# One-bank PSUM tiles and coefficients spread by a product, in a kernel of channel attention and two gated layers

## The chip, the cores and the metric

One core of a Trainium2 chip runs the kernel. The metric is the device time of one execution in microseconds. The engines are PE (matrix products), DVE (vector), ACT (scalar functions), POOL (general) and SP, which only issues loads and stores; each runs its own list of instructions in order. Products write to PSUM, which has eight banks of 512 fp32 columns; everything else lies in SBUF.

## The reference

q, k and v are 6016 x 256. q and k are normalised by column, a 256 x 256 softmax mixes the channels of v, and two layers with a nonlinear gate follow.

```python
qn = q / (np.linalg.norm(q, axis=1, keepdims=True) + 1e-06)
kn = k / (np.linalg.norm(k, axis=1, keepdims=True) + 1e-06)
s = kn.transpose(0, 2, 1) @ qn / tau
a = softmax(s)                       # a /= a.sum(-1) + 1e-09
x = v @ a                            # 6016 x 256
h = x @ w_in                         # 256 -> 2048
P = a[0] + a[1]*h + a[2]*h**2 + a[3]*h**3
Q = 1.0 + abs(b[0])*abs(h) + abs(b[1])*h**2
y = (P / (Q + 1e-06)) @ w_out        # 2048 -> 256
out = (sigmoid(y @ w_gate) * (y @ w_val)) @ w_out2   # 256 -> 1536 -> 256
```

## The kernel before

The weights arrive as 64-bit numbers. Each of 17 pieces (`win0` to `win3`, `wo0` to `wo3`, `wg0` to `wg2`, `wv0` to `wv2`, `wo20` to `wo22`) is loaded, converted to fp32 (`to_f32`: ACT at L710, a shift by DVE at L717 or ACT at L713, a merge of bits by DVE at L721) and split into a high and a low part (`split`: L796 or L800, and the subtraction at L803 by DVE or POOL). Three products of parts then stand for one in fp32.

**Loading.** q and k come in 15 chunks of 2, 4 or 1 tiles of 128 rows (names `<-in_kqk_dram`), into buffers that a weight will take later. PE adds the scores up in `s_ps` (tag `pO`, L489); ACT squares (L510), DVE and POOL add squares (L519), and PE adds them over the rows by products with `ones` into `nrm` (L458). The three coefficient vectors b, tau and a are loaded by SP as broadcasts to 128 partitions (L530), and DVE prepares them (`coefs`, `coefs_a`, L535 to L551).

**Norms and softmax.** DVE adds the sums (L571), ACT takes the root, DVE makes the reciprocals and two diagonal matrices (L584); PE spreads these over the partitions by products with `ones` (L591), DVE copies the result (L593) and makes scaled scores with their maxima (L605), ACT the exponentials, DVE the scale (L622): the weights e (`e_sb`). PE then transposes e (L650) and multiplies the first 384 tokens of v by it (L635, `x_ps`). Filler products that nobody reads (L663, `WARM` of them) keep PE busy.

**Fold.** For the other tokens e is multiplied into w_in: eight units, two to each piece of `win`, of eight instructions each on PE (L754, `w_mm`). ACT evacuates a unit's high part (L766), DVE subtracts for the low part (L768).

**Blocks.** The tokens are worked in 12 blocks, the first of 384, the others of 512. The first layer has eight steps (`moe1`): two first-layer products into `pH` or `pO` (block 0 in plain fp32, L882; later blocks in parts, L872 to L876), the gate on ACT and DVE (u, |h|, h squared, a reciprocal by seed and arctangent; Q at L903, t at L911, y at L916, g at L919), and second-layer products into `pY` (L929 in block 0, L947 to L957 later). `moe2` follows per block (L993 to L1030) beside the next block's first layer.

**PSUM.** Tags `pH`, `pY`, `pO` are tiles of two banks, `pG` and `pV` of one. Until the first product of `moe2`, `pG` and `pV` are the two halves of a single two-bank tile `gv` (class `Half`); then `part_gv` gives it up and opens a pool for each. The norms, the norm product, the fillers, the transposes and the fold units go to these two halves, and in three of block 0's eight steps (`S0`) the squared term `S_` is both halves of `gv` at once. Dependencies are found by tile: an instruction that touches one half of `gv` waits for the users of the other.

**Order.** A planner (`Plan.schedule`) lists the instructions of each engine by modelled ready times and by due times; the tables `VT0`, `VT1`, `VT`, `WT`, `ORDER` and the letter strings set the due times, the order of loads, which engine does a conversion, and which PSUM tile it goes through.

```python
def part_gv():                                        # L343
    if pools["pG"].pool is None:
        both.close()
        for tag in ("pG", "pV"):
            pools[tag].pool = ctx.enter_context(tc.tile_pool(name="r_" + tag, bufs=depth[tag], space=PSUM))
...
for x, lo_, n, k in ((b, 4, 2, "b"), (tau, 6, 1, "t"), (a, 0, 4, "a")):        # L529
    pl.op(SP, .2, -9999.0 + CF_AT["bta".index(k)], lambda x=x, lo_=lo_, n=n: nc.sync.dma_start(
        out=sm[:, lo_:lo_ + n], in_=bcast(x, n)), (), ["sm_" + k], tail=2.0)
```

Of the kernel before, what the change touches and what calls it, by code (L numbers as in the profile page):

```python
# [9 lines left out]
F32 = mybir.dt.float32  # L10
# [4 lines left out]
ALU = mybir.AluOpType  # L15
PSUM = bass.MemoryType.PSUM
# [17 lines left out]
PE, ACT, DVE, POOL, SP = "PE", "ACT", "DVE", "POOL", "SP"  # L34
# [30 lines left out]
WARM = 6  # L65
PLC = (-1, 3, 6, -1, 3, -1, 5, 3, 7, 0, 4, -1, -1, 3, -1)
# [6 lines left out]
TOP = 'adaaaaaddaaddadad'  # L73
HI = 'dadadaadddaaa'
LOW = 'pdppdpdpppppp'


T_PS = 'HYYYH..HYY.YYYY..'
# [12 lines left out]
ET_PS = 'G'  # L91
ET_EV = 'd'
# [184 lines left out]
def tile_channel_attention_two_moes(  # L277
# [14 lines left out]
    nc = tc.nc  # L292
# [30 lines left out]
    class Half:  # L323

        def __init__(self, tag):
            self.tag, self.pool = tag, None

        def tile(self, shape, dtype, tag=None, name=None):
            if self.pool is None:
                return gv[:, "GV".index(self.tag[1]), :]  # L330
            return self.pool.tile(shape, dtype, tag=tag, name=name)

    for tag, n in depth.items():
        if tag in ("pG", "pV"):
            pools[tag] = Half(tag)
            continue
        kw = {"space": PSUM} if tag[0] == "p" else {}
        pools[tag] = ctx.enter_context(tc.tile_pool(name="r_" + tag, bufs=n, **kw))

    both = ctx.enter_context(ExitStack())  # L340
    gv = both.enter_context(tc.tile_pool(name="r_gv", bufs=1, space=PSUM)).tile([P, 2, NB], F32, name="gv")

    def part_gv():  # L343
        if pools["pG"].pool is None:
            both.close()
            for tag in ("pG", "pV"):
                pools[tag].pool = ctx.enter_context(tc.tile_pool(name="r_" + tag, bufs=depth[tag], space=PSUM))
# [178 lines left out]
    def bcast(src, n):  # L526
        return src.rearrange("(o n) -> o n", o=1).broadcast_to([P, n])
# [153 lines left out]
    def to_f32(vt, wt, c, rkey, dst, key, n, how, t_ps, stay=False):  # L681
# [163 lines left out]
    def moe1(b_, y_ps, nat, vhi, vlo, j):  # L845
# [18 lines left out]
        def V(x):  # L864
            return (gv if x is None else x.ap())[:, :, :n]

        for i in range(2):
# [37 lines left out]
            [a_] + S_, [a_], port=not free_s)  # L905
# [69 lines left out]
    def moe2(b_, yhi, ylo):  # L975
# [7 lines left out]
        for f in range(F2):  # L983
# [120 lines left out]
```

## Time and profile before

| | |
|---|---|
| three runs, us | 1220.6, 1221.65, 1222.77 (median 1221.65) |
| the profiled execution, us | 1221.94, span of its instructions 1220.1 |
| mean granted clock of PE | 0.992 |
| busy us: PE, DVE, ACT, POOL | 1186.0, 965.0, 837.8, 510.2 |
| HBM read and written | 36.31 and 6.16 MB |
| loads and stores of SP and ACT | 35 GB/s over the span, but 342, 388 and 272 in the first three slices of 1/40 |

The span runs from the first to the last instruction. A duration in a row is that of the instruction itself; matrix products are pipelined, so a row's products overlap by some 0.1 to 0.2 us with the next row's. The idle time before an instruction is put down to whatever ended it last. On PE a product in fp32 appears as two records.

### The profile page before, as it was taken

To read this page: it belongs to the slowest core of one execution; us is meant where nothing else is said; L and a number is where in the kernel's file an instruction comes from. 1 tells how busy PE (TensorE), PEld (TensorE's weight loads), DVE (VectorE), ACT (ScalarE), POOL (GpSimd) and SP (SyncE) were. 2 spreads that over 40 slices of the span, in tenths; PEclk is the share of its full clock that TensorE was granted. 3 is DMA by queue.
4 is the path that set the end of the run, shared out by engine and by line. 5 is a ranking of instruction groups with operands and counts; after the bars stand their busy time and mean duration, and the time that the engine had idled before them with its cause. 6 is when DMAs were issued, how large, how long until landed. Compare 5 with 4: busy or idle time off the path is not lost.

```text
span 1220.1 us, 13195 instructions
## 1 busy us (share of the span) xinstructions
PE 1186.0 (97%) x5182; PEld 967.6 (79%) x5182; DVE 965.0 (79%) x841; ACT 837.8 (69%) x984; POOL 510.2 (42%) x261
## 2 busy tenths in 40 slices
PE   7978999999999999999999999999999999999998
PEld 5755588888788888888888888888888888888877
DVE  3878988578789789789789889888888878878811
ACT  4787777567677677677677677677677677667622
POOL 2602344444345345345345345345335435435422
PEclk9979999999999999999999999999999999999999
DMA  8970000000100100100100100000000000000000
GB/s 342 388 272 18 18 1 1 31 1 1 35 1 1 35 1 1 35 1 1 35 1 1 35 1 1 27 9 1 18 18 0 18 19 1 18 1 1 18 1 18
DMA packets 15614, 43.32 MB, mean 36 GB/s; under 512 B 1344, under 2 KB 1856, under 8 KB 14272
## 3 DMA queue, kind: packets, MB, share of 16 engines
q1 hardware_dynamic: 15408, 42.21, 9.3%
q8 instruction: 41, 0.67, 0.2%
q10 hardware_dynamic: 144, 0.26, 0.1%
q14 instruction: 21, 0.17, 0.0%
HBM read 36.31 MB, written 6.16 MB: 35 GB/s over the span
## 4 chain that ended last, share of the span: by engine, by line
PE 89%; DVE 5%; DMA 4%; ACT 1%; issue 1%; SPq 0%; DVEq 0%; ACTq 0%
PE pO L1022 10%; PE pY L949 7%; PE pY L947 7%; PE pH L872 6%; PE pH L874 6%; PE pH L876 6%; PE pY L957 6%; PE pG L993 5%; PE pV L993 5%; PE pG L995 5%; PE pV L995 5%; PE pV L997 5%; PE pG L997 5%; PE pO L1030 5%; DMA win<-in_kqk_dram 2%; PE pO L489 1%
## 5 line engine op out<-in xcount | busy, mean ns | idle before, releaser
L1015 POOL TENSOR_TENSOR lo<-sig,hi 128x512 fp32r<-128x512 f32 (+1 forms) x143 | 246.5, 1730 | 333.3 <-ACT hi L1011 333.3
L939 POOL TENSOR_TENSOR lo<-w,hi 128x1024 fp32r<-128x1024 f32 x88 | 216.8, 2463 | 276.9 <-ACT hi L934 229.3
L916 DVE SCALAR_TENSOR_TENSOR a<-a,s 128x1024 f32<-128x1024 f32 (+1 forms) x93 | 162.4, 1748 | 57.5 <-ACT a L913 57.5
L893 ACT ACTIVATE a<-pH,cf 128x1024 f32<-128x1024 f32 (+1 forms) x92 | 101.7, 1106 | 98.5 <-PE pH L876 98.5
L903 DVE SCALAR_TENSOR_TENSOR a<-a,s 128x1024 f32<-128x1024 f32 (+1 forms) x93 | 112.7, 1212 | 49.7 <-ACT s L895 48.1
L1022 PE MATMUL pO<-hi,wo 128*128 128x512 f32 (+1 forms) x580 | 151.5, 383 | 0.0
L913 ACT ACTIVATE a<-a 128x1024 f32<-128x1024 f32 (+1 forms) x96 | 100.0, 1042 | 62.5 <-DVE a L911 61.3
L1008 DVE TENSOR_TENSOR sig<-sig,pV 128x512 f32<-128x512 f32 (+2 forms) x145 | 96.6, 667 | 57.7 <-PE pV L997 54.0
L919 DVE SCALAR_TENSOR_TENSOR w<-w,cf,a 128x1024 f32<-128x1024 f32 (+1 forms) x95 | 138.2, 1456 | 2.9
L947 PE MATMUL pY<-hi,wo 128*128 128x512 f32 x352 | 137.9, 392 | 2.3 <-ACT hi L934 2.3
L872 PE MATMUL pH<-vhi,win 128*128 128x512 f32 x352 | 137.3, 390 | 0.8 <-DVE w L900 0.8
L949 PE MATMUL pY<-hi,wo 128*128 128x512 f32 x352 | 138.0, 392 | 0.0
L911 DVE TENSOR_TENSOR a<-a,s 128x1024 f32<-128x1024 f32 (+1 forms) x89 | 137.9, 1549 | 0.0
L874 PE MATMUL pH<-vlo,win 128*128 128x512 f32 x352 | 137.1, 390 | 0.0
L876 PE MATMUL pH<-vhi,win 128*128 128x512 f32 x352 | 137.1, 389 | 0.0
L1011 ACT ACTIVATE hi<-sig 128x512 fp32r<-128x512 f32 (+2 forms) x145 | 90.3, 623 | 66.1 <-DVE sig L1008 65.8
L1022 PEld LDWEIGHTS pO<-hi,wo 128*128 128x128 f32 x580 | 108.1, 188 | 21.1
L900 DVE SCALAR_TENSOR_TENSOR w<-w,cf,pH 128x1024 f32<-128x1024 f32 (+1 forms) x92 | 116.5, 1266 | 1.7
L993 PE MATMUL pG<-yhi,wg 128*128 128x512 f32 (+1 forms) x288 | 112.1, 389 | 1.6 <-ACT yhi L968 1.1
L995 PE MATMUL pG<-ylo,wg 128*128 128x512 f32 (+1 forms) x288 | 111.2, 386 | 1.5 <-DVE ylo L970 1.5
L1006 ACT ACTIVATE sig<-pG 128x512 f32<-128x512 f32 (+2 forms) x145 | 85.3, 589 | 38.7 <-PE pG L997 24.2
L993 PE MATMUL pV<-yhi,wv 128*128 128x512 f32 (+1 forms) x288 | 111.6, 388 | 0.0
(214 smaller groups left out, 2323.7 us busy)
## 6 DMA issues: line engine op xcount, KB each, us to landing
wo<-in_moe_w_out_dram SPq DMA_DIRECT2D x7, 1024.0 KB, 13.2
v<-in_v_dram SPq DMA_DIRECT2D x11, 512.0 KB, 3.7
out_dram<-v SPq DMA_DIRECT2D x10, 512.0 KB, 2.8
win<-in_kqk_dram SPq DMA_DIRECT2D x4, 1024.0 KB, 14.4
win<-in_moe_w_in_dram SPq DMA_DIRECT2D x4, 1024.0 KB, 8.6
wv<-in_moe_w_val_dram SPq DMA_DIRECT2D x3, 1024.0 KB, 14.1
wo<-in_kqk_dram SPq DMA_DIRECT2D x3, 1024.0 KB, 19.7
wg<-in_moe_w_gate_dram SPq DMA_DIRECT2D x3, 1024.0 KB, 13.8
```

Source lines behind the costliest of these rows:

```text
L872: mm(out=hp.ap()[:, i, :n], lhsT=WIN.at(f * P, 0, z), rhs=vhi.ap()[:, z, :n], start=(z == 0), stop=False)
L874: mm(out=hp.ap()[:, i, :n], lhsT=WIN.at(f * P, 0, z), rhs=vlo.ap()[:, z, :n], start=False, stop=False)
L876: mm(out=hp.ap()[:, i, :n], lhsT=WIN.at(f * P, 1, z), rhs=vhi.ap()[:, z, :n], start=False, stop=(z == 1))
L916: pl.op(DVE, c_dve(N), vt + vp['y'] * d, lambda: stt(out=V(y_), in0=V(a_), scalar=ATAN_C, in1=V(s_), op0=ALU.add, op1=ALU.mult), [a_] + S_ ...
L919: pl.op(DVE, c_dve(N, 1), vt + vp['g'] * d, lambda: stt(out=V(w_), in0=V(w_), scalar=col(A0), in1=V(y_), op0=ALU.add, op1=ALU.mult), [w_, ...
L939: lambda: e_lo.tensor_tensor(out=V(lo), in0=V(w_), in1=V(hi).bitcast(F32), op=ALU.subtract),
L947: mm(out=y_ps.ap()[:, z, :n], lhsT=WO.at(f * C, 0)[:, sl], rhs=hi.ap()[:, i, :n], start=(f == 0), stop=False)
L949: mm(out=y_ps.ap()[:, z, :n], lhsT=WO.at(f * C, 1)[:, sl], rhs=hi.ap()[:, i, :n], start=False, stop=False)
L993: mm(out=gp[i].ap()[:, :n], lhsT=wt.at(f * P, 0, z), rhs=yhi.ap()[:, z, :n], start=(z == 0), stop=False)
L995: mm(out=gp[i].ap()[:, :n], lhsT=wt.at(f * P, 0, z), rhs=ylo.ap()[:, z, :n], start=False, stop=False)
L1015: lambda sg=sg, hi=hi, lo=lo, sl=sl, e=e: e.tensor_tensor(out=lo.ap()[:, sl], in0=sg.ap()[:, sl], in1=hi.ap()[:, sl].bitcast(F32), op=ALU. ...
L1022: mm(out=o_ps.ap()[:, z, sl], lhsT=WO2.at(f * C, i)[:, z * P:(z + 1) * P], rhs=hi.ap()[:, sl], start=(f == 0 and i == 0), stop=False)
```

## The change

`Half`, `gv` and `part_gv` go: `pG` and `pV` are pools of one-bank tiles from the start, so the norms, the norm product, the fillers, the transposes and each fold unit have tiles of their own. The squared term of block 0 always lies in SBUF (`S0`, `W0` go). The coefficients are loaded by ACT as rows into partition 0 of a zeroed tile `row`; one product with `ones` spreads them over the partitions, and DVE copies eight columns. The tables are replaced (`WT`, `VT0`, `VT1`, `UNIT`, `PLC` and others), with twelve fillers instead of six, and the transposes go to a `pO` tile that ACT evacuates.

```diff
-ORDER = 'xx2xvxxxgxvxxxxxgxxoxoiioiongvi22'
+ORDER = 'xx2xxxxxxxgxvvxxogxxxoiiio2nogvi2'
...
-KG = 'ggssssssssssgsg'
+KG = 'ggsssssssssssgs'
...
-S0 = 'sssgsgsg'
-T0 = 'pdpdpppd'
+T0 = 'pdpdpddp'
...
-WARM = 6
+WARM = 12
...
-F_PS = 'VVGGVVGG'
-CF_AT = (4.3, 4.4, 24.5)
+F_PS = 'VVGGVGGV'
...
-ET_PS = 'G'
-ET_EV = 'd'
+ET_PS = 'O'
+ET_EV = 'a'
...
-    class Half:
...
-    both = ctx.enter_context(ExitStack())
-    gv = both.enter_context(tc.tile_pool(name="r_gv", bufs=1, space=PSUM)).tile([P, 2, NB], F32, name="gv")
-
-    def part_gv():
...
-    for x, lo_, n, k in ((b, 4, 2, "b"), (tau, 6, 1, "t"), (a, 0, 4, "a")):
-        pl.op(SP, .2, -9999.0 + CF_AT["bta".index(k)], lambda x=x, lo_=lo_, n=n: nc.sync.dma_start(
-            out=sm[:, lo_:lo_ + n], in_=bcast(x, n)), (), ["sm_" + k], tail=2.0)
+    row = const.tile([P, 8], F32, name="row")
+    pl.op(POOL, .2, t_s - 1, lambda: nc.gpsimd.memset(row, 0.0), (), ["row"], port=True)
+    for x, lo_, n, k in ((a, 0, 4, "a"), (b, 4, 2, "b"), (tau, 6, 1, "t")):
+        pl.op(ACT, .1, -30000.0, lambda x=x, lo_=lo_, n=n: nc.scalar.dma_start(
+            out=row[0:1, lo_:lo_ + n], in_=x.rearrange("(o n) -> o n", o=1)), ["row"], ["row_" + k], tail=9.0)
+    c_ps = pl.buf("pG", [P, 512], at=t_s)
+    pl.op(PE, .1, -30000.0, lambda: mm(out=c_ps.ap()[:, 0:8], lhsT=ones, rhs=row, start=True, stop=True),
+          ["ones", "row", "row_a", "row_b", "row_t"], [c_ps])
+    pl.op(DVE, .2, -30000.0, lambda: nc.vector.tensor_copy(sm[:, 0:8], c_ps.ap()[:, 0:8]), [c_ps],
+          ["sm_a", "sm_b", "sm_t"])
...
-        free_s = b_ == 0 and S0[j] == "g"
-        if free_s:
-            S_ = [pl.buf("pG", [P, 512], at=at), pl.buf("pV", [P, 512], at=at)]
-            s_ = None
-        else:
-            s_ = pl.buf("s", [P, 2, NB], at=at)
-            S_ = [s_]
+        s_ = pl.buf("s", [P, 2, NB], at=at)
+        S_ = [s_]
```

Three places of the lists follow; a number behind a name is that of the buffer, and L numbers are those of each kernel's own file. The start of PE's list: products of the scores (`pO`) and of the sums (`gv` or `pV`, out of `s` and `a`), and the spreading of `row`. Before:

```order
L489 MATMUL pO_134<-wg0_126 128x384 x4
L458 MATMUL gv_112<-ones_114,s_132 128x1 x4
L489 MATMUL pO_134<-wv1_128 128x384 x4
L458 MATMUL gv_112<-ones_114,a_139 128x1 x4
L489 MATMUL pO_134<-win0_141 128x256 x8
```

Now:

```order
L464 MATMUL pO_141<-wo20_133 128x384 x4
L433 MATMUL pV_156<-ones_116,s_139 128x1 x4
L507 MATMUL pG_164<-row_119,ones_116 128x8
L464 MATMUL pO_141<-wv0_135 128x384 x4
L433 MATMUL pV_156<-ones_116,a_148 128x1 x4
L464 MATMUL pO_141<-wo0_137 128x256 x8
```

The product of the coefficients stands between the first and the second chunk.

SP's list around the last chunks of q and k (`in_kqk_dram`). Before:

```order
L413 DMA wv2_309<-in_kqk_dram 128x2048
L413 DMA win3_317<-in_kqk_dram 128x512
L413 DMA wo0_321<-in_moe_w_out_dram 128x4x512
L413 DMA wo22_340<-in_kqk_dram 128x512
L413 DMA wo1_343<-in_moe_w_out_dram 128x4x512
L413 DMA wg1_361<-in_moe2_w_gate_dram 128x2x1024
L413 DMA win1_379<-in_kqk_dram 128x512
```

Now:

```order
L388 DMA wo0_303<-in_moe_w_out_dram 128x4x512
L388 DMA wg1_314<-in_moe2_w_gate_dram 128x2x1024
L388 DMA wv1_329<-in_moe2_w_val_dram 128x2x1024
L388 DMA wo2_344<-in_kqk_dram 128x2048
L388 DMA wv2_355<-in_kqk_dram 128x512
L388 DMA wg2_360<-in_kqk_dram 128x512
L388 DMA win1_365<-in_kqk_dram 128x512
```

Seven weights stood ahead of the last chunk, now six do.

PE's list from the sums to the first products of block 0: the norm product (out of `w` and `ones`, 128x128), fillers (128x256), the transposes (with `ident`), the product with v (`v` and `a`), fold units (`hi` or `vhi` with `v`), and first-layer products (out of `vlo`). Before:

```order
L591 MATMUL gv_112<-w_418,ones_114 128x128 x2
L663 MATMUL gv_112<-w_418,ones_114 128x256 x6
L650 MATMUL gv_112<-ident_113,a_479 128x128 x4
L635 MATMUL pH_510<-v_463,a_479 128x384 x4
L754 MATMUL gv_112<-hi_434,v_513 128x256 x4
L754 MATMUL gv_112<-vhi_454,v_513 128x256 x4
L882 MATMUL pH_549<-vlo_530,hi_434 128x384 x2
L754 MATMUL gv_112<-hi_434,v_513 128x256 x4
```

Now:

```order
L570 MATMUL pG_466<-w_439,ones_116 128x128 x2
L642 MATMUL pV_473<-w_439,ones_116 128x256 x6
L614 MATMUL pH_504<-v_470,a_479 128x384 x4
L629 MATMUL pO_519<-ident_115,a_479 128x128 x4
L642 MATMUL pV_473<-w_439,ones_116 128x256
L854 MATMUL pH_533<-vlo_524,hi_452 128x384 x2
L731 MATMUL pG_541<-vhi_487,v_529 128x256 x4
L854 MATMUL pH_533<-vlo_524,hi_452 128x384 x2
L854 MATMUL pO_560<-vlo_524,hi_452 128x384 x4
```

The product with v has moved ahead of the transposes, the first first-layer products ahead of the fold, and the names of the tiles differ from unit to unit; five more fillers follow further down.

## Rows read from the trace of the kernel before

**Rows 1.** Stretches: length, busy us (instructions) by engine, PE's clock, DMA share, GB/s.

```profile
12.00:18.00 6.00, 5.15 (x27) 4.12 (x25) 0.38 (x3) 3.74 (x5) 2.36 (x1) 1.00 0.67 235
18.00:58.00 40.00, 34.77 (x157) 29.53 (x158) 29.69 (x31) 28.25 (x30) 23.93 (x10) 1.00 1.01 404
58.00:64.50 6.50, 6.50 (x48) 5.98 (x46) 6.10 (x9) 5.81 (x6) 0.09 (x1) 0.90 0.80 269
64.50:77.70 13.20, 7.20 (x21) 5.25 (x21) 9.10 (x28) 9.43 (x13) 0.00 (x0) 0.53 1.01 395
77.70:83.80 6.10, 6.10 (x24) 4.64 (x25) 4.11 (x4) 4.84 (x6) 2.74 (x1) 1.00 0.96 358
83.80:112.30 28.50, 22.43 (x81) 14.51 (x79) 21.10 (x26) 22.45 (x29) 6.83 (x3) 1.00 0.07 23
112.30:148.70 36.40, 34.73 (x108) 20.19 (x109) 36.05 (x39) 29.36 (x37) 11.87 (x6) 1.00 0.05 15
227.00:1220.10 993.10, 983.70 (x4314) 809.31 (x4312) 791.61 (x647) 673.13 (x789) 425.69 (x213) 1.00 0.03 12
```

The engines in a row stand in the order PE, PE's weight loads, DVE, ACT, POOL.

**Rows 2.** Loads and stores: who issues, count, KB each, us from issue to landing.

```profile
out_dram<-v ACTq DMA_DIRECT2D x1, 256.0 KB, 2.1
sm<-in_moe_b_dram SPq DMA_DIRECT2D x1, 1.0 KB, 13.7
...
sm<-in_moe_a_dram SPq DMA_DIRECT2D x1, 2.0 KB, 8.1
```

**Rows 3.** PE in order of time: start, duration, line, product, records, [idle before <-releaser].

```profile
9.98 2.83 PE L489 MATMUL pO<-wv 128*128 128x384 f32 x8
...
40.35 3.62 PE L489 MATMUL pO<-wo 128*128 128x256 f32 x16
...
57.70 1.45 PE L489 MATMUL pO<-wo 128*128 128x384 f32 x4
...
63.50 0.99 PE L458 MATMUL gv<-ones,s 128*128 128x1 f32 x4
69.74 1.22 PE L591 MATMUL gv<-w,ones 128*128 128x128 f32 x4 [5.25 <-DVE w L584]
...
72.33 4.63 PE L663 MATMUL gv<-w,ones 128*128 128x256 f32 x10 [0.52 <-DVE w L593]
...
77.67 2.85 PE L635 MATMUL pH<-v,a 128*128 128x384 f32 x8 [0.24 <-DVE hi L721]
80.35 1.89 PE L754 MATMUL gv<-hi,v 128*128 128x256 f32 x8
...
83.81 1.45 PE L882 MATMUL pH<-vlo,hi 128*128 128x384 f32 x4
...
143.12 5.43 PE L929 MATMUL pY<-w,hi 128*128 128x384 f32 x16 [0.62 <-DVE w L919]
```

**Rows 4.** DVE in order of time, from the sums to block 0's last gate product.

```profile
66.51 0.17 DVE L542 TENSOR_SCALAR cf<-sm 128x4 f32<-128x4 f32 x1 [1.81 <-DMA sm<-in_moe_a_dram]
...
71.86 0.42 DVE L593 COPY w<-gv 128x256 f32<-128x256 f32 x1 [1.91 <-PE gv L663]
72.20 1.22 DVE L721 SCALAR_TENSOR_TENSOR lo<-pY,win 128x1024 int32<-128x1024 int32 x1
...
76.13 0.35 DVE L622 TENSOR_SCALAR a<-a,sm 128x256 f32<-128x256 f32 x1
...
143.97 1.02 DVE L919 SCALAR_TENSOR_TENSOR w<-w,cf,gv 128x768 f32<-128x768 f32 x1
```

**Rows 5.** DVE by line, 76 to 145 us: busy, mean ns | idle before, releasers.

```profile
L768 DVE TENSOR_TENSOR win<-gv,win 128x512 fp32r<-128x512 f32 x8 | 5.5, 689 | 7.8 <-PE gv L754 4.1 <-ACT win L766 3.0 <-ACT wo L713 0.7
L916 DVE SCALAR_TENSOR_TENSOR a<-a,s 128x768 f32<-128x768 f32 x5 | 4.7, 950 | 0.0
```

**Rows 6.** DVE in order of time: two instructions that run beside POOL.

```profile
55.74 3.43 DVE L721 SCALAR_TENSOR_TENSOR ylo<-ylo,wo 128x1024 int32<-128x1024 int32 x1 [0.15 <-ACT wo L713]
...
177.31 2.04 DVE L911 TENSOR_TENSOR a<-a,s 128x1024 f32<-128x1024 f32 x1
```

More of the change, by code (lines that the diff above doesn't have):

```diff
@@ L49 @@
 LOADS = (2, 2, 4, 4, 4, 4, 4, 4, 4, 4, 4, 4, 1, 1, 1)
-KG = 'ggssssssssssgsg'
-UNIT = 'ddpddpdpddpppppddppdddppdpddppp'
+KG = 'ggsssssssssssgs'
+UNIT = 'dppppdpddpppdppddpppddpdpppdpdp'
 IN_TMP = ('hi', 'vhi', 'lo', 'lo')
-TMP = ('yhi', 'ylo', 'v', 'hi', 'lo', 'v', 's', 'vlo', 'vhi', 'v', 's', 'w', 'lo')
-LO0 = 'dpdppdpd'
-S0 = 'sssgsgsg'
-T0 = 'pdpdpppd'
+TMP = ('yhi', 'ylo', 'v', 'hi', 'vhi', 'v', 's', 'w', 'w', 'hi', 'ylo', 'a', 'hi')
+LO0 = 'dppppddp'
+T0 = 'pdpdpddp'
 HAM = 0.5
 SUM_AT = 1
-WARM = 6
@@ L66 @@
-PLC = (-1, 3, 6, -1, 3, -1, 5, 3, 7, 0, 4, -1, -1, 3, -1)
+WARM = 12
+PLC = (0, 2, -1, 7, 0, 6, -1, 2, -1, -1, -1, 6, -1, 7, 2)
 ACTIVE = 0.5
@@ L70 @@
 DEPTH = {'w': 3, 'a': 3, 's': 2, 'hi': 2, 'lo': 2, 'sig': 2, 'hi2': 2, 'lo2': 2, 'yhi': 1, 'ylo': 1, 'vhi': 1, 'vlo': 1, 'v': 2, 'pH': 1, 'pG': 1, 'pV': 1, 'pY': 1, 'pO': 1}
[L73 to L78, printed above, removed]
+TOP = 'aaaadadddddaaadad'
+HI = 'dddaaaaadddda'
+LOW = 'ddpdppppppddp'
+T_PS = 'YYYY.H..HY.Y.YH..'
 VLO = 'dpd'
 YR = 'rrrr'
-X_PS = 'ppppppspppspp'
-W0 = 'gsssgsgg'
-FO_AT = -5.0
-F_PS = 'VVGGVVGG'
-CF_AT = (4.3, 4.4, 24.5)
+X_PS = 'sspppppssppsp'
+FO_AT = 0.0
+F_PS = 'VVGGVGGV'
 X0_AT = 'vlo'
@@ L322, in tile_channel_attention_two_moes @@
     pools = {}
-    class Half:
[L325 to L331, printed above, removed]
     for tag, n in depth.items():
-        if tag in ("pG", "pV"):
-            pools[tag] = Half(tag)
-            continue
         kw = {"space": PSUM} if tag[0] == "p" else {}
         pools[tag] = ctx.enter_context(tc.tile_pool(name="r_" + tag, bufs=n, **kw))
-    both = ctx.enter_context(ExitStack())
-    gv = both.enter_context(tc.tile_pool(name="r_gv", bufs=1, space=PSUM)).tile([P, 2, NB], F32, name="gv")
-    def part_gv():
[L344 to L347, printed above, removed]
     ident = const.tile([P, P], F32, name="ident")
@@ L482, in tile_channel_attention_two_moes @@
         dma(turn("x", c), lambda kq=kq: kq.ap(), kqk[:, t0:t0 + n, :], n * 2 * C * 4 * P, (), [kq], 421e3,
-            0.55 if c == 1 else 0.0)
+            0.0)
         def s_mm(kq=kq, n=n, c=c):
@@ L692, in to_f32 @@
             ts = [(d, [key], 0, wt.shapes()[c][0])]
-        elif t_ps == "2":
-            ts = [(None, [pl.buf("pG", [P, 512], at=at), pl.buf("pV", [P, 512], at=at)])]
         else:
@@ L705, in tv @@
                     return d(t)
-                f = (gv if t_ps == "2" else tt[0].ap()).rearrange("p a c -> p (a c)")
+                f = tt[0].ap().rearrange("p a c -> p (a c)")
                 return f[:, :n // len(ts)].rearrange("p (a n) -> p a n", a=half).bitcast(t)
@@ L864, in V @@
         def V(x):
-            return (gv if x is None else x.ap())[:, :, :n]
+            return x.ap()[:, :, :n]
         for i in range(2):
@@ L904, in moe1 @@
             out=V(a_), in0=V(a_), scalar=1.000001, in1=V(s_), op0=ALU.add, op1=ALU.add),
-            [a_] + S_, [a_], port=not free_s)
+            [a_] + S_, [a_], port=True)
         pl.op(ACT, c_act(N, 0), vt + vp['seed'] * d, lambda: act(
@@ L908, in moe1 @@
             [a_], S_)
-        t_pool = b_ == 0 and T0[j] == "p" and not free_s
+        t_pool = b_ == 0 and T0[j] == "p"
         e_t = nc.gpsimd if t_pool else nc.vector
         pl.op(POOL if t_pool else DVE, c_pool(N) if t_pool else c_dve(N), vt + vp['t'] * d, lambda: e_t.tensor_tensor(
-            out=V(a_), in0=V(a_), in1=V(s_), op=ALU.mult), [a_] + S_, [a_], port=not free_s)
+            out=V(a_), in0=V(a_), in1=V(s_), op=ALU.mult), [a_] + S_, [a_], port=True)
         pl.op(ACT, c_act(N, 0), vt + vp['at'] * d, lambda: act(
             out=V(a_), in_=V(a_), func=ACTF.Arctan, scale=ATAN_S, bias=ATAN_B), [a_], [a_])
-        y_, Y_ = (s_, S_) if free_s and W0[j] == "g" else (a_, [a_])
+        y_, Y_ = a_, [a_]
         pl.op(DVE, c_dve(N), vt + vp['y'] * d, lambda: stt(
             out=V(y_), in0=V(a_), scalar=ATAN_C, in1=V(s_), op0=ALU.add, op1=ALU.mult),
-            [a_] + S_, Y_, port=not free_s)
+            [a_] + S_, Y_, port=True)
         pl.op(DVE, c_dve(N, 1), vt + vp['g'] * d, lambda: stt(
             out=V(w_), in0=V(w_), scalar=col(A0), in1=V(y_), op0=ALU.add, op1=ALU.mult),
-            [w_, "cf_a"] + Y_, [w_], port=y_ is a_)
+            [w_, "cf_a"] + Y_, [w_], port=True)
         if plain_y:
@@ L990, in g_mm @@
                 def g_mm(i=i, wt=wt, gp=gp, f=f):
-                    part_gv()
                     for z in range(2):
```

8 lines of the change are left out of this document (3 added, 5 removed).

## The prediction

> **What bounds the kernel now.** I read the table of stretches first. From the second block on (227 us to the end) PE is busy 983.70 of 993.10 us at full clock, and the lists of instructions agree row for row on all five engines from the middle of block 1 on. That part can only move as a whole, so the prediction is about the first 148.55 us, up to the end of block 0's last second-layer product at 143.12 + 5.43 [rows 1, 3]. There the bound changes three times.
>
> Loading (to 59.1 us). From 18 to 58 us the DMA engines move 404 GB/s at a share of 1.01: they are the bound. They fall to 235 GB/s from 12 to 18 us and to 269 from 58 to 64.5 us [rows 1]. The broadcast loads of the coefficients lie there. That of b is sixth in SP's list and takes 13.7 us to land; that of a takes 8.1 us, and DVE waits for it until 66.51 us [rows 2, 4]. Their 1 and 2 KB cannot fill that time by size; each is 128 tiny pieces in the queue of the large loads. The last product of the scores ends at 57.70 + 1.45 = 59.1 us [rows 3].
>
> Norms and softmax (59.1 to 77.67 us). The list of DVE in time shows it idle 1.81 us for the load of a before it may touch the finished sums, and idle 1.91 us before it copies the norms, behind a filler product that writes the other half of the same tile [rows 4]. PE waits 5.25 us; from 64.5 to 77.7 us the granted clock is 0.53 on average, so nearly all of that stretch runs at 1.2 GHz [rows 1, 3].
>
> Fold and block 0 (77.7 to 148.55 us). From 112.3 to 148.7 us DVE is busy 36.05 of 36.40 us: it is the bound. From 83.8 to 112.3 us it is busy only 21.10 of 28.50 us [rows 1], and 7.8 us of idle time stand in front of the eight fold subtractions alone, ended by fold products (4.1 us) and by ACT's evacuation (3.0 us) [rows 5]. Each fold unit needs its own half of the tile only; as one tile, it waits for the readers of the other half too.
>
> **Loading after the change.** (1) The three broadcasts leave SP's queue. Valuing the dips at the rate beside them, the first cost 6 x (404 - 235) / 404 = 2.5 us ahead of the last chunk; the second, 6.5 x (404 - 269) / 404 = 2.2 us, delays only the loads behind it. (2) In SP's list six weight loads instead of seven stand ahead of the last chunk: 1.05 MB at 404 GB/s, 2.6 us. So the scores end 5.1 us earlier, at 54.0. PE could keep that pace: from 9.98 + 2.83 + 0.9 = 13.7 us ten chunks of 3.62 us [rows 3] make 49.9, with 3 us of small chunks 52.9. (3) On ACT the three new loads stand ahead of its first square, which cannot start before chunk 0 lands; that wait covers their issue, and without it they would delay the squares by their issue alone. POOL gets one small memset. (4) PE gets a new wait: the product that spreads the coefficients stands behind chunk 0 and ahead of chunk 1, and every other product of the scores is queued behind it. PE reaches it at about 10 us [rows 3]. No row shows a one-partition load at this time. The nearest are 2.1 us (an output store on ACT's queue, little else moving) and 13.7 us (b, behind five loads, 4 MB, of SP's queue) [rows 2]. Issued near 2 us it lands between 4 and 16 us: a stall of 0 to 6 us. I take 0, because b's time is that of the loads ahead of it in its own queue and ACT's queue holds nothing else; the other end is a rival. The DMA: Bandwidth & Descriptors page of the Trainium skill (Issuing engines are not separate DMA queues) says that loads issued from several engines run on the same 16 DMA engines and interleave, so that only issue time is saved. By that rule the new queue gains no bandwidth, the small loads may still wait behind large ones, and the sum would go by the rival's price, 1216; no run here shows two queues at once.
>
> **Norms after the change.** The sums end at 63.50 + 0.99 = 64.5 now [rows 3]; 59.4 after. The 1.81 us for a go. But DVE's list has several conversions queued ahead of the sums, so I do not credit it whole: PE's wait goes from 5.25 to 4.0 us (2.5 to 5.25), and the norm product starts at 63.4. The fillers no longer share a tile with the norms (0.9 us), and the bit merge that stands between the copy of the norms and the scores (1.13 us at 72.20) moves behind them; against it ACT takes one conversion between the two exponentials. From 69.74 to the end of the softmax scale (76.13 + 0.35) it is 6.7 us now [rows 3, 4]; I take 5 (4 to 6.7), so the weights e are ready at 68.4. PE's list has six of the fillers ahead of the product with v. At half clock one takes 4.63 / 5 = 0.93 us [rows 3]: 63.4 + 1.2 + 5.6 = 70.2 us, later than e. So the product with v starts at 70.2 instead of 77.67, 7.4 us earlier. The transposes now follow it, and the first first-layer product stands ahead of the fold instead of behind two units of it (83.81 - 80.35 = 3.5 us): 74.0 against 83.81.
>
> **Fold and block 0 after the change.** DVE, from e ready to its last gate product: busy 1.2 + 4.1 + 21.1 + 32.3 = 58.7 us of the 68.5 us between 76.48 and 144.99 [rows 1, 4]. Its list has 69 rows there now instead of 65: the extra ones are conversions, 3.5 us in all (0.7 us for a shift, as the fold's 0.689 us [rows 5], about 1.2 us for a merge or a subtraction, as at 72.20 [rows 4]). Idle time is 9.8 us now, 7.8 of it in front of the fold. With own tiles for the units I leave 5 us (2 to 10): 68.4 + 62.2 + 5 = 135.6 against 145.0. From DVE's end to the end of the last second-layer product is 3.6 us: 139.2. PE as a check: busy 22.43 + 34.73 + 3.5 = 60.7 us from the first fold unit on [rows 1, 3], plus five more fillers at full clock (0.93 / 2 each, 2.3 us): 74.0 + 63.0 = 137 at the earliest. The fillers stand ahead of a fold unit whose evacuation ACT reaches later anyway, and cost nothing while that holds; 2.3 us otherwise. **Sum:** 148.6 to 139.1, 9.5 us earlier.
>
> In three of the eight steps of block 0 the squares now lie in SBUF instead of PSUM, so ten more DVE instructions read two SBUF operands. Beside POOL a product of 1,024 columns took 2.04 us where 0.950 us for 768 columns makes 1.27, and a merge 3.43 where it takes 1.22 alone [rows 4 to 6]. I take 1 us, inside the idle time above, since such instructions of block 0 show the 0.950 us now; the ends are 0 and 10 x 0.77 = 7.7. SBUF — State Buffer of the Trainium skill (Who interferes with whom) says that a DVE instruction with two SBUF inputs contends with a GpSimd one that reads SBUF. The row of 2.04 us agrees. It speaks against the change: by that rule for all ten the gain would shrink to 9.5 - 7.7 = 1.8 us, 1220.
>
> The profiled execution took 1221.94 us with a span of 1220.1; the median of the runs is 0.3 lower: 1221.65 - 9.5 = 1212.1.
>
> **Rivals.**
> A. Forecast: both false waits go, block 0 ends 9.5 us earlier: 1212, own range 1207 to 1216. For it: DVE is idle where readers of the other half end the wait. Chance 0.66.
> B. The coefficients land as late as b does. PE starts chunk 1 at 16 instead of 10 us and becomes the bound of the loading: 52.9 + 6 = 58.9 instead of 54.0 (the rows overlap a little, so 3 to 5 us later): 1216. Against it: nothing is ahead of them in their queue. Chance 0.13.
> C. The waits around the fold are true ones, for weights and for ACT, which is as full there as DVE (22.45 of 28.50 us [rows 1]). All 9.8 us of idle time come back, 5 us more than taken: 1217. Chance 0.09.
> D. No change (within 0.2%, 2.4 us, about what a measurement of this kernel can tell): extra conversions and collisions eat the gain, 1220. Chance 0.05.
> E. Slower: DVE, the bound of block 0, is held by POOL whenever it reads two SBUF operands. At the merge's full hold, 3.43 - 1.22 = 2.2 us, the ten new ones cost 22 us at most; from the fifth on (11 us) the kernel is slower, and with seven 15.4 - 9.5 = 6 us slower: 1228. For it: the rows of 2.04 and 3.43. Against it: the 0.950 us. Chance 0.07.
>
> **How the numbers follow.** The likeliest is A: 1212. The range leaves out D, E and the ends of A and C: 1206 to 1219. Faster by over 0.2% are A, B and C, 0.88; same 0.05; slower 0.07.
>
> **What would show it.** Right: DMA near 400 GB/s through 12 to 18 us, the scores ending near 54, the product with v near 70, the first first-layer product near 74, under 4 us of DVE idle time in front of the fold subtractions, block 0's last second-layer product ending near 139, and the same stretch from 227 us on, moved. Wrong: PE waiting over 2 us at the coefficients' product (B), DVE waiting as now around the fold (C), DVE's products of block 0 above 1.1 us beside POOL (E), or a gain in the loading that is gone by 148 us.

## The result and the profile after

The changed kernel took 1209.88 us (median of four runs, 1207.88 to 1211.5) against 1221.29 us: ratio 0.9904, interval 0.9884 to 0.9924. Forecast were 1212.0 us and 1206 to 1219. The profiled execution took 1208.7 us with a span of 1206.9.

The steps that the prediction names, in us from the start of the span; the ends are start plus duration of the rows below:

| | before | forecast | after |
|---|---|---|---|
| last product of the scores ends | 59.1 | 54.0 | 55.1 |
| last of the sums ends | 64.5 | 59.4 | 62.1 |
| norm product starts | 69.7 | 63.4 | 64.1 |
| weights e ready | 76.5 | 68.4 | 69.5 |
| product with v starts | 77.7 | 70.2 | 68.9 |
| first first-layer product starts | 83.8 | 74.0 | 72.8 |
| DVE's last gate product of block 0 ends | 145.0 | 135.6 | 133.6 |
| last second-layer product of block 0 ends | 148.6 | 139.1 | 137.2 |

The last line gained 11.4 us, as much as the medians. The rest only moved: from that line to the end of the span it is 1071.5 us before, 1069.7 after, and 1070.4 to 1072.0 in the twelve runs below, a scatter that follows no edit. So the line tells where in an execution a gain came from. It is the line of one execution, though (the changed kernel's own two profiles have 137.2 and, in e12, 136.2), so the prices below are taken from the medians.

The table of stretches of the changed kernel (us busy and instructions by engine, granted clock, DMA share, GB/s), to be read against [rows 1]:

```profile
12.00:18.00 6.00, 6.00 (x31) 4.90 (x31) 5.12 (x7) 4.11 (x6) 5.84 (x3) 1.00 0.97 359
18.00:55.00 37.00, 34.22 (x158) 29.43 (x156) 28.06 (x26) 28.57 (x30) 25.93 (x12) 1.00 1.02 409
55.00:64.00 9.00, 7.15 (x45) 7.06 (x43) 7.41 (x17) 6.14 (x8) 0.06 (x1) 0.63 1.03 394
64.00:74.00 10.00, 9.76 (x34) 7.00 (x35) 8.44 (x21) 9.66 (x15) 0.00 (x0) 0.82 1.04 401
74.00:100.00 26.00, 23.98 (x95) 17.43 (x94) 25.05 (x29) 24.26 (x31) 8.95 (x4) 1.00 0.17 65
100.00:137.20 37.20, 36.14 (x119) 21.98 (x117) 36.84 (x41) 29.02 (x35) 9.42 (x5) 1.00 0.10 29
```

The two holes of the DMA rate (235 and 269 GB/s) are nearly filled (359 and 394 now), and DVE is nearly full from 74 us on (25.05 of 26.00 us), where it was idle 7.4 of 28.5 us. PE's list in time, with the idle time before a row and what ended it:

```profile
10.54 0.37 PE L507 MATMUL pG<-row,ones 128*128 128x8 f32 x2
...
48.35 3.72 PE L464 MATMUL pO<-wo 128*128 128x256 f32 x16 [2.79 <-DMA wo<-in_kqk_dram]
...
54.06 1.03 PE L464 MATMUL pO<-win 128*128 128x256 f32 x4
54.92 1.84 PE L433 MATMUL pV<-ones,w 128*128 128x1 f32 x16
...
60.30 1.84 PE L433 MATMUL pV<-ones,s 128*128 128x1 f32 x8
64.09 1.22 PE L570 MATMUL pG<-w,ones 128*128 128x128 f32 x4 [1.94 <-DVE w L563]
65.10 3.95 PE L642 MATMUL pV<-w,ones 128*128 128x256 f32 x12
68.93 2.85 PE L614 MATMUL pH<-v,a 128*128 128x384 f32 x8
...
72.80 1.56 PE L854 MATMUL pH<-vlo,hi 128*128 128x384 f32 x4
...
131.75 5.43 PE L901 MATMUL pY<-w,hi 128*128 128x384 f32 x16 [1.04 <-DVE w L891]
```

The product that spreads the coefficients (10.54) has no wait before it. PE waits 1.94 us for the norms, 5.25 before [rows 3]. DVE's list in time:

```profile
62.19 0.16 DVE L550 TENSOR_TENSOR sm<-sm,pV 128x4 f32<-128x4 f32 x1 [1.18 <-PE pV L433]
...
65.35 0.43 DVE L572 COPY w<-pG 128x256 f32<-128x256 f32 x1 [1.06 <-PE pG L570]
...
69.18 0.35 DVE L601 TENSOR_SCALAR a<-a,sm 128x256 f32<-128x256 f32 x1
...
132.60 1.02 DVE L891 SCALAR_TENSOR_TENSOR w<-w,cf,a 128x768 f32<-128x768 f32 x1
```

The wait for a is gone, the copy of the norms waits for the norm product and for no filler, and the eight fold subtractions have no idle time before them (7.8 us before, [rows 5]). Seven of them, from 82 us on (the first, at 77.90, has none either): count | busy, mean ns | idle before:

```profile
L745 DVE TENSOR_TENSOR win<-pV,win 128x512 fp32r<-128x512 f32 x4 | 2.7, 684 | 0.0
L745 DVE TENSOR_TENSOR win<-pG,win 128x512 fp32r<-128x512 f32 x3 | 2.0, 682 | 0.0
```

### The profile page after: what moved, and what is told of

Same layout as the page of the kernel before. It is cut to its first block, busy times and chain, and to the rows that moved or that the text cites. A ratio compares the mean times of both kernels' runs of the same rounds, so it can differ in the third digit from the quotient of the medians.

```text
span 1206.9 us, 13209 instructions
## 1 busy us (share of the span) xinstructions
PE 1183.8 (98%) x5192; PEld 968.9 (80%) x5192; DVE 968.8 (80%) x842; ACT 836.9 (69%) x983; POOL 513.4 (43%) x264
## 4 chain that ended last, share of the span: by engine, by line
PE 91%; DVE 4%; ACT 2%; DMA 1%; issue 1%; POOL 1%; DVEq 0%; SPq 0%; ACTq 0%
PE pO L993 10%; PE pH L844 7%; PE pH L846 7%; PE pH L848 7%; PE pY L921 6%; PE pY L919 6%; PE pY L929 6%; PE pG L964 5%; PE pG L966 5%; PE pV L964 5%; PE pG L968 5%; PE pV L966 5%; PE pV L968 5%; PE pO L1001 5%; PE pO L464 3%; DMA wo<-in_kqk_dram 1%
## 5 line engine op out<-in xcount | busy, mean ns | idle before, releaser
L888 DVE SCALAR_TENSOR_TENSOR a<-a,s 128x1024 f32<-128x1024 f32 (+1 forms) x96 | 166.5, 1736 | 58.5 <-ACT a L885 58.5
L875 DVE SCALAR_TENSOR_TENSOR a<-a,s 128x1024 f32<-128x1024 f32 (+1 forms) x96 | 115.9, 1208 | 50.0 <-ACT s L867 48.3
L891 DVE SCALAR_TENSOR_TENSOR w<-w,cf,a 128x1024 f32<-128x1024 f32 (+1 forms) x96 | 139.1, 1452 | 2.8
L883 DVE TENSOR_TENSOR a<-a,s 128x1024 f32<-128x1024 f32 (+1 forms) x92 | 139.5, 1517 | 0.0
L919 PE MATMUL pY<-hi,wo 128*128 128x512 f32 x352 | 137.2, 390 | 2.3 <-ACT hi L906 2.3
L848 PE MATMUL pH<-vhi,win 128*128 128x512 f32 x352 | 137.2, 390 | 0.0
L846 PE MATMUL pH<-vlo,win 128*128 128x512 f32 x352 | 137.2, 390 | 0.0
## 6 DMA issues: line engine op xcount, KB each, us to landing
wg<-in_moe_w_gate_dram SPq DMA_DIRECT2D x3, 1024.0 KB, 12.3
```

The costliest lines, as they stand in the source:

```text
L846: mm(out=hp.ap()[:, i, :n], lhsT=WIN.at(f * P, 0, z), rhs=vlo.ap()[:, z, :n], start=False, stop=False)
L848: mm(out=hp.ap()[:, i, :n], lhsT=WIN.at(f * P, 1, z), rhs=vhi.ap()[:, z, :n], start=False, stop=(z == 1))
L888: pl.op(DVE, c_dve(N), vt + vp['y'] * d, lambda: stt(out=V(y_), in0=V(a_), scalar=ATAN_C, in1=V(s_), op0=ALU.add, op1=ALU.mult), [a_] + S_ ...
L919: mm(out=y_ps.ap()[:, z, :n], lhsT=WO.at(f * C, 0)[:, sl], rhs=hi.ap()[:, i, :n], start=(f == 0), stop=False)
```

## The experiments

Theory: two needless waits made the time, those of a tile shared by halves and those behind the broadcast loads, and the new tables only make use of what they left. Rivals: the new order itself is the gain; DVE's collisions with POOL take it back. In every run but e4 the lists of all engines are those of the changed kernel except for the edit. Ratios are to the kernel before, measured beside each. The changed kernel has 0.9904, and 0.9910 when run again (e12, at the end), so a price is given against both.

**e1, the two-bank tile back.**

```diff
+        if tag in ("pG", "pV"):
+            pools[tag] = Half(tag)
...
+    gv = both.enter_context(tc.tile_pool(name="r_gv", bufs=1, space=PSUM)).tile([P, 2, NB], F32, name="gv")
```

> The changed kernel with one thing undone: the two one-bank tiles are again the two halves of one two-bank tile until the first gate product. Every engine's list stays as it is. Theory (false waits): the copy of the norms waits again for a filler, about 0.9 us, and the eight fold subtractions have up to 7.8 us of DVE idle time in front of them again, as in the kernel before; DVE is the bound of block 0, so 4 to 8 us come back: 1214 to 1218 us, ratio to the kernel before 0.994 to 0.997, last second-layer product of block 0 ending at 141 to 145 instead of 137.2. Rival (the new order did it): the lists are already such that no half waits for the other's readers: within 1 us of the changed kernel, ratio 0.990 to 0.991.

Measured 0.9982 (0.9971 to 0.9992), 1219.55 us: 8.8 to 9.5 us come back, a little more than the theory's upper end. PE's list:

```profile
65.81 1.06 PE L664 MATMUL gv<-w,ones 128*128 128x256 f32 x2
67.39 4.64 PE L664 MATMUL gv<-w,ones 128*128 128x256 f32 x10 [0.52 <-DVE w L594]
71.82 3.56 PE L636 MATMUL pH<-v,a 128*128 128x384 f32 x8
...
140.01 5.43 PE L923 MATMUL pY<-w,hi 128*128 128x384 f32 x16 [1.00 <-DVE w L913]
```

and of DVE the copy of the norms, then the group of the fold subtractions (busy, mean ns, idle before and what ended it):

```profile
66.91 0.42 DVE L594 COPY w<-gv 128x256 f32<-128x256 f32 x1 [1.91 <-PE gv L664]
```
```profile
L767 DVE TENSOR_TENSOR win<-gv,win 128x512 fp32r<-128x512 f32 x8 | 5.4, 686 | 5.4 <-ACT win L765 3.9 <-PE gv L664 1.5
```

The copy waits 1.91 us behind a filler, and the other five fillers wait for the copy, so they run at half clock ahead of the product with v, which starts 2.9 us later than in the changed kernel (0.7 of it were there at the norm product already). The first-layer product is 3.6 us late, the end of block 0 (145.4) 8.3 us: the difference of 4.7 us arises behind it, where the fold subtractions have 5.4 us of idle time in front of them and none in the changed kernel.

**e2, the broadcasts back.** The three loads have their old due times in SP's list, which puts b behind four loads (3 MB) where it was behind five (4 MB); the rest is undone as its expectation says.

```diff
+        LATE = [(at, lambda x=x, lo_=lo_, n=n: nc.sync.dma_start(
+            out=sm[:, lo_:lo_ + n], in_=x.rearrange("(o n) -> o n", o=1).broadcast_to([P, n])))
+                for x, lo_, n, at in ((b, 4, 2, 4.3), (tau, 6, 1, 4.4), (a, 0, 4, 24.5))]
```

> The changed kernel with one thing undone: the three broadcast loads are back on SP's queue at their old places, the spreading product and its copy are gone, and the scaling of a stands again just ahead of the addition of the sums; all else keeps its order. Theory: the DMA rate falls to 235 GB/s or so between 12 and 18 us and again near the load of a, the last product of the scores ends 2.5 us later (near 57.5 instead of 55.1), and DVE waits up to 2 us for a; 2.5 to 4.5 us come back: 1212 to 1214.5, ratio 0.992 to 0.9945. Rival (the loads are hidden, block 0 has room for them): within 1 us of the changed kernel, ratio 0.990 to 0.991.

Measured 0.9939 (0.9926 to 0.9952): 3.5 to 4.3 us, as the theory had it, but in part in another way. Two stretches of the table, a load (KB, us to landing), and a row of PE's list:

```profile
10.00:12.00 2.00, 2.00 (x8) 1.21 (x7) 0.00 (x0) 1.52 (x3) 1.79 (x1) 1.00 0.04 0
...
50.00:55.00 5.00, 5.00 (x12) 3.96 (x13) 4.96 (x6) 4.61 (x7) 2.36 (x2) 0.50 1.05 399
```
```profile
sm<-in_moe_b_dram SPq DMA_DIRECT2D x1, 1.0 KB, 9.8
```
```profile
49.99 6.41 PE L464 MATMUL pO<-wo 128*128 128x256 f32 x16 [5.67 <-DMA wo<-in_kqk_dram]
```

For 2 us, at 10 to 12 and not at 12 to 18 (386 GB/s there), the DMA engines move nothing, and b, issued at 2.59, lands just behind, at 12.4. The last large chunk of the scores starts 1.64 us later (49.99 against 48.35; the nine profiles with the rows and these lists have 47.60 to 48.62). While PE waits 5.67 us for it the granted clock falls to 0.50, and the chunk takes 6.41 instead of 3.72 us: 2.69 us more. But in e1, e6 and e7, which have the rows, PE waits 3.11 to 3.57 us and the chunk takes 5.41 us, so only 1.0 us is more than happens without broadcasts; how much of the price is the clock's stays open. The load of a stalls nobody here, and its 2 KB, issued at 47.6 and landed at 59.9 us, make no such hole: 399 GB/s from 50 to 55 us, 340 from 57 to 62.

**e3, both back, only the new tables left.**

> Both undone, only the new tables are left. Theory (the tables by themselves bring little): the two prices add, 6.5 to 11 us come back: 1216.5 to 1221, ratio 0.996 to 1.000. Rival (the new order is the gain): at most 2 us come back, ratio 0.990 to 0.992.

Measured 0.9998 (0.9986 to 1.001): the whole gain is gone, 10.7 to 11.5 us. The rival falls: the new order alone is worth nothing that can be measured. Block 0 in its profile:

```profile
140.10 5.43 PE L922 MATMUL pY<-w,hi 128*128 128x384 f32 x16 [1.01 <-DVE w L912]
```

That end, 145.5, is 3.0 us ahead of the kernel before, but this execution (1218.45 us) was the second fastest of twelve, which reach 1223.79. The two prices do not add: undone one at a time they come to 12.3 to 13.8 us. With the other part undone already, the two-bank tile costs 7.2 us (e3 against e2) and the broadcasts 2.0 (e3 against e1, whose intervals overlap).

**e4, the old tables with both parts.** The three steps that had s in the two-bank tile get one tile of their own in SBUF.

```diff
-            return (gv if x is None else x.ap())[:, :, :n]
+            return (s3 if x is None else x.ap())[:, :, :n]
```

> The kernel before, its tables and the order of every engine kept, with both parts of the change: one-bank tiles (s of the three steps that had it in the two-bank tile lies in a tile of SBUF of its own) and the coefficients as rows, spread by the product with ones. Theory: most of the gain comes without the new tables, 5 to 9 us: 1212 to 1216, ratio 0.993 to 0.996; DVE idle in front of the fold subtractions under 4 us (7.8 before), last second-layer product of block 0 ending at 139.5 to 143.5 instead of 148.55. Rival (the new order is the gain): 0 to 2 us, ratio 0.998 to 1.000.

Measured 0.9921 (0.9909 to 0.9934), 1211.79 us: 9.7 us of the gain without one entry of the tables; block 0 ends at 139.56, and the fold subtractions have 0.3 us of idle time:

```profile
134.13 5.43 PE L938 MATMUL pY<-w,hi 128*128 128x384 f32 x16 [0.62 <-DVE w L928]
```
```profile
L777 DVE TENSOR_TENSOR win<-pG,win 128x512 fp32r<-128x512 f32 x4 | 2.7, 686 | 0.3 <-ACT win L775 0.3
L777 DVE TENSOR_TENSOR win<-pV,win 128x512 fp32r<-128x512 f32 x4 | 2.7, 683 | 0.0
```

What is missing against the changed kernel is 1.3 to 2.1 us, inside both intervals. The trace shows a place where it could be lost. DVE, then POOL:

```profile
118.10 2.06 DVE L920 TENSOR_TENSOR a<-a,s 128x768 f32<-128x768 f32 x1
120.08 0.95 DVE L925 SCALAR_TENSOR_TENSOR a<-a,s 128x768 f32<-128x768 f32 x1
121.06 1.02 DVE L928 SCALAR_TENSOR_TENSOR w<-w,cf,a 128x768 f32<-128x768 f32 x1
122.00 2.03 DVE L925 SCALAR_TENSOR_TENSOR a<-a,s 128x768 f32<-128x768 f32 x1
124.06 1.91 DVE L928 SCALAR_TENSOR_TENSOR w<-w,cf,a 128x768 f32<-128x768 f32 x1
```
```profile
116.99 2.35 POOL L812 TENSOR_TENSOR wo<-lo,wo 128x1024 fp32r<-128x1024 f32 x1
121.95 3.21 POOL L849 TENSOR_TENSOR vlo<-v,vhi 128x512 fp32r<-128x512 f32 x2 [2.60 <-issue]
```

Three products that read two SBUF operands take twice their time where POOL works beside them; with one of 2.41 us at 102.55 they lose 4.5 us against 0.95 and 1.02 undisturbed. SBUF — State Buffer of the Trainium skill (Who interferes with whom) says that such instructions contend with those of GpSimd (POOL) that read SBUF; these rows agree. In the changed kernel the longest product of that width in block 0 is 1.29 us; most of what DVE does there beside POOL reads PSUM. So the tables seem to keep POOL's work away from the new SBUF operands; that this is the missing 1.3 to 2.1 us is read from the rows of two traces, and no run shows it.

**e5, the rows issued by SP.**

```diff
-        pl.op(ACT, .1, -30000.0, lambda x=x, lo_=lo_, n=n: nc.scalar.dma_start(
+        LATE = [(at, lambda x=x, lo_=lo_, n=n: nc.sync.dma_start(
             out=row[0:1, lo_:lo_ + n], in_=x.rearrange("(o n) -> o n", o=1)))
```

> The changed kernel, but its three one-partition loads are issued by SP, behind the fifth chunk of the scores' input and ahead of the first weight load, instead of by ACT at the start. Two theories of what made the broadcasts dear. By the place (rival B's price): whatever stands behind the large loads lands when they have landed, here after some 4 MB, so near 13 to 14 us; the spreading product holds PE from about 10.5 us on for 2.5 to 4 us and the scores end up to 3 us later: 1211 to 1213, ratio 0.992 to 0.994, DMA rate between 10 and 16 us as in the changed kernel. By the pieces (128 of them for each broadcast, in which the queue moves nothing for about 2 us): three single pieces cost nothing in the queue, no stretch of the first 18 us is lower than in the changed kernel, but the wait of PE is the same. If they land before 10.5 us instead, both fall and the time is that of the changed kernel, 0.990 to 0.991.

Measured 0.9897 (0.9884 to 0.991): no price. They stood behind four chunks of 3 MB, not five. PE:

```profile
10.05 1.34 PE L433 MATMUL pV<-ones,s 128*128 128x1 f32 x8
11.25 0.37 PE L506 MATMUL pG<-row,ones 128*128 128x8 f32 x2
```

They landed before PE came to them, and from 10 to 12 us the rate was 418 GB/s, where the broadcasts of e2 at the same place had 0. The pieces were dear, not the place.

**e6, without the fillers.** The products at L642 are left out; nothing reads their results.

> The changed kernel without its twelve filler products, whose results nothing reads. As forecast (twelve fillers cost nothing and bring nothing that is on the path): the product with v starts at 68.9 as now, since it waits for the weights e, and the time is within 1.5 us of the changed kernel, ratio 0.989 to 0.992. Rival (they are there for the clock): without them PE is idle from 65.3 to 68.9 us, the granted clock stays at 0.5 through the product with v and the first first-layer product, which together take 4 us longer; DVE waits for them and 2 to 4 us come back, ratio 0.992 to 0.994.

Measured 0.9937 (0.9925 to 0.9949): 3.3 to 4.0 us slower than the changed kernel; the rival holds. PE:

```profile
65.41 1.23 PE L570 MATMUL pG<-w,ones 128*128 128x128 f32 x4 [1.94 <-DVE w L563]
70.25 5.49 PE L614 MATMUL pH<-v,a 128*128 128x384 f32 x8 [3.62 <-DVE sm L599]
```

Idle for 3.62 us, PE is still at 0.50 through the product with v: 5.49 instead of 2.85 us. e7's profile, whose norm product starts at the same time (65.48) with the fillers in place, ends block 0 at 138.57, this one at 141.08.

**e7 and e8, the one-column sums broken up.** e7 moves the last chunk of the scores behind the first group of the sums; e8 adds 4 + 3 fillers of 128 columns.

```diff
             o.fn()
+            if o is first_acc:
+                s_last.fn()
+            if o in FILL:
+                fill(FILL[o])
```

> The changed kernel with one product moved on PE: the last chunk of the scores (1.03 us) runs behind the first group of the sums instead of ahead of it, so that a product of 256 columns lies among the products of one column. Theory: the one-column products do not hold the clock (it fell 2.4 us after they began, at 57.3), and from there to the norm product PE is the path; the clock falls later, the last sum ends 0.5 to 1.5 us earlier than 62.15, ratio 0.989 to 0.990. Rival: the clock falls at the same time, or the sums wait for their inputs anyway: no change, 0.990 to 0.991.

> As the run before, and in addition four filler products of 128 columns behind the second group of the sums and three behind the last, ahead of the norm product. Theory: the clock stays at 2.4 GHz or comes back before the norms; fillers (4 x 0.22 us) cost less than the sums and the norm product gain (3.5 us at half clock instead of 1.7): the norm product starts near 62.5 instead of 64.1, ratio 0.988 to 0.990. Rival: the clock falls nevertheless, the four fillers cost 1.8 us at half clock: the norm product starts near 65.5, ratio 0.991 to 0.993.

Measured 0.9901 (0.9885 to 0.9917) and 0.9915 (0.9900 to 0.9931): no gain from either. In e7's profile the clock had already fallen in the last large chunk, so it says nothing of the theory; in e8's it had not, the norm product starts at 62.39 and block 0 ends at 135.75. But e12, the changed kernel without these fillers, has 62.48 in its profile, and by the ratios e8 is no faster than e12. That the half clock of the sums costs time is shown by the rows (8 records at 60.30 take 1.84 us, as long as the 16 at 54.92); that fillers mend it is not.

**e9, the broadcasts at the start, issued by ACT.**

```diff
-            out=row[0:1, lo_:lo_ + n], in_=x.rearrange("(o n) -> o n", o=1)))
+            out=sm[:, lo_:lo_ + n], in_=x.rearrange("(o n) -> o n", o=1).broadcast_to([P, n])))
```

> The changed kernel, but ACT issues at the start, in place of the three one-partition loads, the three broadcast loads of the kernel before (128 pieces each) straight into the tile of the coefficients; the spreading product and its copy are gone. Which part made the broadcasts dear: their pieces or SP's queue? Pieces that hold the DMA engines themselves: the hole of about 2 us shows up again in the first 18 us (a stretch of 2 us under 200 GB/s that the changed kernel does not have), the scores end 1.5 to 4 us later, 1211.5 to 1214, ratio 0.992 to 0.994. Only the loads behind them in the same queue are held: no hole, the time of the changed kernel, 0.989 to 0.991.

Measured 0.9919 (0.9905 to 0.9932), 1.1 to 1.8 us slower than the changed kernel, inside the intervals and just under what the pieces should cost. The trace shows it more plainly. The hole is there, at another time (a stretch of the table), and ACT's first square starts at 6.14, 1.49 us later than in the changed kernel:

```profile
4.00:6.00 2.00, 0.00 (x0) 0.00 (x0) 0.00 (x0) 0.00 (x0) 0.00 (x0) 1.00 0.69 218
```
```profile
6.14 0.63 ACT L485 ACTIVATE s<-wo 128x512 f32<-128x512 f32 x1 [2.71 <-DMA wo<-in_kqk_dram]
```

The changed kernel moves 420 GB/s in that stretch; from 2 to 4 us it is 162 against 313. So the broadcasts hold up large loads of the other queue too. DMA: Bandwidth & Descriptors of the Trainium skill (Issuing engines are not separate DMA queues) says that loads issued by several engines run on the same 16 DMA engines and interleave; this run agrees (the first square 1.49 us later). By the medians the price is less than half of e2's; since place and queue change together here, why it is less stays open.

**e10, e11 and e12, fillers in the gap before the last large chunk.** e10 puts ten products of 128 columns there, e11 adds those of e8; e12 is the changed kernel again.

```diff
+            if o is s_ops[11]:
+                gap.append(pools["pG"].tile([P, 512], F32, tag="pG", name="pG"))
+                for _ in range(10):
+                    mm(out=gap[0][:, 0:P], lhsT=ones, rhs=ident, start=True, stop=True)
```

> The changed kernel with ten more filler products of 128 columns (2.2 us) on PE ahead of the last large chunk of the scores, where PE is idle 2.3 to 3.6 us for its load. Theory: that idle time decides whether the clock falls; where it falls the chunk takes 5.4 instead of 3.7 us (seen in the profiles of five of the eight runs so far, in the changed kernel's own profile not). With the fillers the chunk takes 3.7 us, the runs lie together at the lower end of the changed kernel's, 1207.5 to 1209, ratio 0.988 to 0.990. Rival: the clock falls later in any case (the one-column sums follow) and only the place differs: 1209 to 1211, 0.990 to 0.991.

> Both kinds of fillers and the moved product: ten products of 128 columns ahead of the last large chunk, the last chunk behind the first group of the sums, four fillers behind the second group and three ahead of the norm product. Theory: scores at full clock, norm product near 62.4 instead of 64.1, end of block 0 near 135.8: 1206 to 1208.5, ratio 0.987 to 0.989. Rival: the seven later fillers cost what they bring: the same as with the ten alone.

> The changed kernel itself once more, as the measure beside the three others on the same chip. Ratio 0.989 to 0.992, single runs from 1207.5 to 1212, in two groups: where the last large chunk takes 3.7 us and where it takes 5.4.

The count in the first of these is off: in six of the eight profiles of experiments the clock fell at that chunk, in e8 it did not, and e4 has no such gap. Measured: 0.9901 (0.9887 to 0.9914), 0.9912 (0.9897 to 0.9926) and 0.9910 (0.9894 to 0.9926). e10's PE:

```profile
45.11 2.40 PE L1041 MATMUL pG<-ident,ones 128*128 128x128 f32 x20
47.60 3.72 PE L464 MATMUL pO<-wo 128*128 128x256 f32 x16
```

The chunk takes 3.72 us, as expected. That the fillers bring the runs together is not shown: e10's four lie at 1208.53 to 1209.75, but the five of e11, whose chunk takes 3.72 us too, at 1209.06 to 1213.31, nearly as wide as the nine of the changed kernel (1207.88 to 1213.39). e11's forecast, 1206 to 1208.5, is missed: its norm product starts at 65.45. No median moves beyond the interval, so no version here beats the changed kernel. e12's PE, the same program as the changed kernel:

```profile
58.33 1.03 PE L433 MATMUL pV<-ones,s 128*128 128x1 f32 x8
62.48 1.22 PE L570 MATMUL pG<-w,ones 128*128 128x128 f32 x4 [3.11 <-DVE w L563]
```

Here the granted clock is 1.00 through the sums, which end at 59.4, and falls behind them.

## Why the prediction was right

The forecast A was the mechanism, and the rivals are settled by runs: the new order as such (e3), late coefficients (B; no wait at 10.54), true waits around the fold (C; e4 and the changed kernel have 0.3 us or less there), POOL's holds (E; under 1 us in this kernel's products). The time came out 2.1 us under the forecast. The steps were off in both directions and cancel in part, which is luck:

- **Loading (1), (2).** 4.0 of the 5.1 us came. PE did not keep the pace without a gap: it waits 2.79 us for the last large chunk. From 12 to 18 us the rate rose to 359 GB/s, not to the 404 that the forecast took: 0.7 us of that stretch (an estimate) was not the broadcasts' doing.
- **Wait for the coefficients (4).** Taken as 0, measured 0. The reason given, that b's landing was the time of the loads ahead of it, is half true: in e2 the loads ahead of it are through at 10 us, and it lands at 12.4, after the hole that its own pieces make; rows at that place land in time (e5).
- **Norms.** Two errors cancel. The sums end 2.7 us later than forecast, because the scores end 1.1 us late and the clock falls at 57 us, when PE has gone over to the one-column sums; PE's wait is 1.94 instead of 4.0. The norm product is 0.7 us off. In e12's profile, where the clock falls only behind the sums, they end at 59.4, as forecast, and the wait is 3.11.
- **Fillers.** A step that failed. I had six of them hold the product with v until 70.2 us and the others cost 0 or 2.3 us. They ended at 69.0, no later than the weights, and they bring the clock back: without them 3.3 to 4.0 us are lost (e6).
- **Fold and block 0.** DVE is busy 62.56 of the 64.10 us from 69.5 to 133.6; forecast were 62.2 busy and 5 idle. This term carried most of the miss: idle time was 1.5 us.
- **POOL.** 1 us taken. In block 0 the nine products at L875, eight at L888 and four at L883 have means of 1.04 (one of them has 1,024 columns), 0.95 and 0.95 us, against 0.95 undisturbed: under 1 us for these products; a merge of a conversion (2.02 us at 79.63) lost 0.8. The other end, 7.7 us, was possible: e4 lost 4.5.

## What to carry to other kernels

A tile that is shared by halves makes waits between work that shares nothing, and the profile shows it as idle time ended by an instruction on the other half; here it was 7 to 9.5 of 11 us. Two broadcasts to 128 partitions, 1.5 KB together, stopped the DMA engines for 2 us among large loads (e2), and all three slowed them at the start (e9), though a's alone, later, made no such hole; rows spread by a product cost nothing measurable. A filler that delays nothing may still be worth its place through the clock: leave it out once and measure.

## What was not expected of the hardware

- The gap before the last large chunk and the clock. After gaps of 2.58, 2.79 and 2.98 us the chunk took 3.72 us (clock 1.00), after 3.11 to 4.58 us 5.41 (clock 0.50 in part), but after 2.35 us (e5) 5.28. The length of the gap alone does not decide it.
- Instructions of DVE with one to four columns, beside POOL. The scaling of a (128 x 4) took 2.26 us and a product of one column 2.25 us while POOL added squares (11.10 to 18.3 us); the same kind takes 0.15 us alone. Nobody waited for them here.
